# Load order and row length in a cached-attention kernel: K0 between the halves of wq, K further ahead of V, three pairs of V chunks in 32 KB rows

## The chip, the cores and the metric

One core of a Trainium2 chip. The metric is the device time of one execution in microseconds. The profile shows a span some 1.8 us shorter than that time; the stretches and moments below are in microseconds from the start of the span. The record marks each run fast or slow by its time and granted clock.

## The reference, cut to what matters

One query token per sequence, 32 sequences, 32 query heads over 8 K/V heads, a window of the last 512 cached positions, heads of 128, everything in bfloat16:

```python
q = (x @ wq).reshape(B, Sq, Hq, Dh).transpose(0, 2, 1, 3)   # x [32, 1, 512], wq [512, 4096]
k = repeat(k_cache[:, :, Sk - W:, :], 4, axis=1)            # k_cache [32, 8, 2048, 128], W = 512
v = repeat(v_cache[:, :, Sk - W:, :], 4, axis=1)
p = softmax(einsum("bhqd,bhkd->bhqk", q, k) * Dh ** -0.5)
o = einsum("bhqk,bhkd->bhqd", p, v).reshape(B, Sq, Hq * Dh) @ wo   # wo [4096, 512]
```

The used window of the two caches is 67 MB, the weights 8.4 MB. Each K and V element is used for four query rows, so there is little arithmetic per byte.

## The kernel before: the parts that matter

K and V come in 16 chunks each. A chunk is 2 MB: 128 partitions of 16 KB. Two neighbouring chunks, 2q and 2q+1, belong to the same four sequences, and in memory the two 16 KB rows of a partition touch. K has 3 buffers (`NK`), V has 4 (`NV`). wq comes in two 2 MB halves, wo at the end in 4 KB rows. All these loads go through one queue, in the order of a list, and each waits for its buffer:

```python
DMA_ORDER = (
    "K0 K1 K2 V0 K3 K4 V1 K5 K6 K7 V2 K8 K9 V3 K10 V4 K11 K12 V5 K13 K14 V6 K15 V7 V8 V9 V10 V11 V12 "
    "V13 V14 V15"
).split()
def cache_rows(cache, m):
    q, e = divmod(m, 2)
    rows = cache[4 * q:4 * q + 4, :, SK - W:, :].rearrange("b g (s r) d -> (b g) s (r d)", s=KS)
    return rows[:, :, e * CR * DH:(e + 1) * CR * DH]
...                                       # first both halves of wq, then in the order of the list:
    if name[0] == "K":
        if n >= NK:
            sp.wait_ge(dve_T, 2 * (n - NK + 1))       # both transposes of K(n-3) are done
        sp.dma_start(K_sb[:, n % NK]..., cache_rows(k_cache, n)).then_inc(sem_k[n % NK], 16)
    else:
        if n >= NV:
            sp.wait_ge(pe_PV, n - NV + 1)             # PV of V(n-4) is done
        sp.dma_start(V_sb[:, n % NV]..., cache_rows(v_cache, n)).then_inc(sem_v[n % NV], 16)
...
sp.wait_ge(pe_PV, 2 * Z_HOME.rindex("w") + 2)         # PV 11 is done: wo may overwrite w_sb
```

Every engine walks its own list. On VectorE, `Tn.b` transposes half b of chunk Kn, `Mq` and `Rq` are the row maximum and the inverse sum of a softmax, `Zq.i` is a quarter of the spread of the probabilities over a block-diagonal operand (multiplies with a mask; ScalarE does another share of it). On TensorE, `Sq` are the scores of chunks 2q and 2q+1, `Pq` turns the probabilities, `Vn` multiplies chunk Vn ("PV n"). On ScalarE, `E`, `N`, `C`, `O` are the exponential, the normalisation and two evacuations. GpSimd builds the scores' weight operand. In the profile's lines PE is TensorE (PEld its weight loads), DVE VectorE, ACT ScalarE, POOL GpSimd, and SPq the queue from which SyncE issues the loads.

Of the kernel before, what the change touches and what calls it, by code (L numbers as in the profile page):

```python
# [12 lines left out]
def bass_standalone__sliding_block_cached__sampling_kernel(  # L13
# [7 lines left out]
):  # L21
    B, Sq, D = x.shape
    _, HKV, SK, DH = k_cache.shape
    HD = wq.shape[1]
    HQ = HD // DH
# [8 lines left out]
    U32 = mybir.dt.uint32  # L34
    NK = 3
    NV = 4
# [4 lines left out]
    CR = KR // 2  # L41
# [6 lines left out]
    ZD = XD // 4  # L48
    ZA = (NBG - XD) // 4
    DMA_ORDER = (  # L50
        "K0 K1 K2 V0 K3 K4 V1 K5 K6 K7 V2 K8 K9 V3 K10 V4 K11 K12 V5 K13 K14 V6 K15 V7 V8 V9 V10 V11 V12 "
        "V13 V14 V15"
    ).split()
    PE_ORDER = (
        "S0 P0 S1 P1 V0 V1 S2 P2 V2 S3 V3 S4 P3 P4 V4 S5 V5 P5 S6 V6 P6 V7 S7 V8 V9 P7 V10 V11 V12 V13 "
        "V14 V15"
    ).split()
    DVE_ORDER = (
        "T0.0 T0.1 T1.0 T1.1 T2.0 T2.1 M0 R0 T3.0 Z0.0 T3.1 Z0.1 T4.0 M1 Z0.2 R1 T4.1 Z0.3 T5.0 T5.1 "
        "T6.0 T6.1 Z1.0 Z1.1 M2 Z1.2 R2 T7.0 Z1.3 T7.1 T8.0 T8.1 M3 T9.0 R3 T9.1 Z2.0 T10.0 M4 Z2.1 R4 "  # L60
        "T10.1 Z2.2 Z2.3 T11.0 T11.1 T12.0 T12.1 M5 R5 Z3.0 T13.0 Z3.1 T13.1 Z3.2 T14.0 M6 Z3.3 R6 T14.1 "
        "Z4.0 T15.0 Z4.1 T15.1 Z4.2 Z4.3 Z5.0 M7 Z5.1 Z5.2 R7 Z5.3 Z6.0 Z6.1 Z6.2 Z6.3 Z7.0 Z7.1 Z7.2 "
        "Z7.3"
    ).split()
    ACT_ORDER = (
        "E0 N0 C0 Z0.0 Z0.1 Z0.2 Z0.3 E1 N1 C1 O0 Z1.0 Z1.1 E2 Z1.2 N2 Z1.3 C2 E3 N3 O1 Z2.0 Z2.1 C3 E4 "
        "Z2.2 N4 Z2.3 C4 E5 N5 O2 Z3.0 C5 Z3.1 Z3.2 Z3.3 E6 N6 Z4.0 Z4.1 C6 Z4.2 Z4.3 O3 Z5.0 Z5.1 E7 "
        "Z5.2 N7 Z5.3 Z6.0 Z6.1 C7 O4 Z6.2 Z6.3 Z7.0 Z7.1 O5 Z7.2 Z7.3 O6 O7"
    ).split()
    Z_HOME = "wwwwkwtk"  # L70

    with ExitStack() as es:
        sb = lambda name, shape, dt: es.enter_context(nc.sbuf_tensor(name, shape, dt))
# [3 lines left out]
        w_sb = sb("w_sb", [P, DKT, HD], BF16)  # L77
        K_sb = sb("K_sb", [P, NK, CR, DH], BF16)
        KT_sb = sb("KT_sb", [P, NK, 2, G, CR, KS, 2], BF16)
        V_sb = sb("V_sb", [P, NV, CR, DH], BF16)  # L80
# [14 lines left out]
        Q_sb = KT_sb[:, 2].rearrange("p b i r s e -> p (b i r s e)")[:, 0:8 * DH].rearrange("p (h d) -> p h d", h=8)  # L95
# [7 lines left out]
        QW = oT_flat.bitcast(U32).rearrange("p (h k b) -> p h k b", h=8, k=2)  # L103
        QA = QA_sb[:, :, :, :, :, :].rearrange("p c h q k e -> p (c h q k e)").bitcast(U32).rearrange(
            "p (c h q k) -> p c h q k", c=4, h=8, q=NQUAD)
# [12 lines left out]
        X_ps = ps("X_ps", [P, 3, 512], F32)  # L118
# [3 lines left out]
        sem_wq = [sem(f"sem_wq{i}") for i in range(2)]  # L122
# [3 lines left out]
        sem_v = [sem(f"sem_v{i}") for i in range(NV)]  # L126
        sem_out = sem("sem_out")
        pe_xT = sem("pe_xT")
        pe_q = sem("pe_q")
        pe_S = sem("pe_S")  # L130
        pe_PT = sem("pe_PT")
        pe_PV = sem("pe_PV")
# [3 lines left out]
        dve_q = sem("dve_q")  # L136
# [6 lines left out]
        act_q = sem("act_q")  # L143
# [15 lines left out]
        wq_rows = wq.rearrange("(p t) n -> p (t n)", t=DKT)  # L159
        wq_half = DKT * HD // 2  # L160
# [9 lines left out]
        def pos_half(q, e):  # L170
            return e ^ kt_pair(q)[2]

        def z_of(q):
            return {"w": Z_w, "k": Z_k, "t": Z_t}[Z_HOME[q]]

        def z_waits(eng, q):
            if q == 0:
                eng.wait_ge(pool_mask, 3)
                eng.wait_ge(pe_q, 1)
            elif Z_HOME[q] in Z_HOME[:q]:  # L180
                eng.wait_ge(pe_PV, 2 * Z_HOME[:q].rindex(Z_HOME[q]) + 2)
            elif Z_HOME[q] == "k":
                eng.wait_ge(dve_T, 2 * NCH - 2)
            else:
                eng.wait_ge(pe_S, NQUAD)

        def cache_rows(cache, m):
            q, e = divmod(m, 2)
            rows = cache[4 * q:4 * q + 4, :, SK - W:, :].rearrange("b g (s r) d -> (b g) s (r d)", s=KS)
            return rows[:, :, e * CR * DH:(e + 1) * CR * DH]  # L190

        @block.sync
        def _(sp):
            sp.dma_start(
                w_sb[:, 2:4, :].rearrange("p k n -> p (k n)"), wq_rows[:, wq_half:]
            ).then_inc(sem_wq[1], 16)
            for name in DMA_ORDER:
                n = int(name[1:])
                if name[0] == "K":
                    if n >= NK:  # L200
                        sp.wait_ge(dve_T, 2 * (n - NK + 1))
                    sp.dma_start(  # L202
                        K_sb[:, n % NK].rearrange("p r d -> p (r d)"), cache_rows(k_cache, n)
                    ).then_inc(sem_k[n % NK], 16)
                else:
                    if n >= NV:
                        sp.wait_ge(pe_PV, n - NV + 1)
                    sp.dma_start(
                        V_sb[:, n % NV].rearrange("p r d -> p (r d)"), cache_rows(v_cache, n)
                    ).then_inc(sem_v[n % NV], 16)  # L210
            sp.wait_ge(pe_PV, 2 * Z_HOME.rindex("w") + 2)
            for hg in range(NHG):
                for i0, i1 in ((0, 4),) if hg < NHG - 1 else ((0, WO_CUT), (WO_CUT, 4)):
                    sp.dma_start(  # L214
                        wo_sb[:, hg, i0:i1].rearrange("p i n -> p (i n)"),
                        wo[hg * 512:(hg + 1) * 512, :].rearrange("(m i) n -> m (i n)", i=4)[:, i0 * 512:i1 * 512],
                    ).then_inc(sem_last if i0 else sem_wo[hg], 16)
            sp.wait_ge(dve_out, 2)
            sp.wait_ge(act_out, 2)
            sp.dma_start(  # L220
                out.rearrange("b s n -> b (s n)"), out_sb[:, :, :].rearrange("b c n -> b (c n)")
            ).then_inc(sem_out, 16)
            sp.wait_ge(sem_out, 16)
# [58 lines left out]
        def _(pe):  # L282
# [64 lines left out]
            def pv(m):  # L347
                q, e = divmod(m, 2)
                pe.wait_ge(dve_Z, q + 1)
                pe.wait_ge(act_Z, q + 1)  # L350
                if q >= 2 and e == 0:
                    pe.wait_ge(act_O, q - 1)
                pe.wait_ge(sem_v[m % NV], 16 * (m // NV + 1))
                x0 = CR * pos_half(q, e)
                for r in range(CR):
                    ins = pe.matmul(  # L356
                        O_ps[:, q % 2, 0:P],
                        lhsT=V_sb[:, m % NV, r, :],
                        rhs=z_of(q)[:, :, x0 + r, :],
                        start=(e == 0 and r == 0), stop=(e == 1 and r == CR - 1), tile_position=(0, 0),  # L360
                    )
                ins.then_inc(pe_PV, 1)
# [13 lines left out]
            for name in PE_ORDER:  # L376
                k = int(name[1:])
# [25 lines left out]
        def _(dve):  # L403
# [1 line left out]
            dve.tensor_copy(  # L405
                xT_sb[:, :, :], X_ps[:, 2, 0:DKT * 32].rearrange("p (kt b) -> p kt b", b=32)
            ).then_inc(dve_xT, 1)
            dve.wait_ge(pe_q, 1)
            dve.tensor_copy(  # L409
                Q_sb[:, 0:4, :].rearrange("p h d -> p (h d)"), X_ps[:, 0, :]  # L410
            ).then_inc(dve_q, 1)
            dve.wait_ge(dve_q, 1)
            dve.wait_ge(act_q, 1)
            dve.transpose(  # L414
                QW.rearrange("p h k b -> p (h k b)"),
                Q_sb[:, :, :].rearrange("p h d -> p (h d)").bitcast(U32),
            ).then_inc(dve_q, 1)
            dve.wait_ge(dve_q, 2)
            for a in range(4):
                for c in range(4):  # L420
                    dve.tensor_copy(  # L421
                        QA[32 * a:32 * a + 32, c],
                        QW[32 * c:32 * c + 32, :, :, a::4].rearrange("p h k q -> p h q k"),
                    ).then_inc(dve_q, 1)

            def turn(n, b):
                if b == 0:
# [32 lines left out]

            for name in DVE_ORDER:
                arg = [int(a) for a in name[1:].split(".")]
                {"T": turn, "M": top, "R": inverse, "Z": spread}[name[0]](*arg)

            def sel_evac(src, i0, ni, b0, b1):
                return (
# [111 lines left out]
```

## Time and profile before

| | before |
|---|---|
| time, median of 3 runs | 187.71 us (187.68 to 188.07) |
| span of the profile | 185.9 us |
| DMA, mean over the span | 408 GB/s |
| VectorE busy | 131.9 us (71%) |
| TensorE busy | 109.0 us (59%), granted clock 0.85 |
| packets | 6304 |

The row to read first is the busy share of the DMA engines over the 40 slices (the prediction below shows it): it stands at 9 from the second slice to the 38th. The packets of the kernel before:

```profile
DMA packets 6304, 75.80 MB, mean 408 GB/s; under 512 B 720, under 2 KB 912, under 8 KB 1936
```

34 loads of 2 MB with 128 rows each make 4352, the nine wo loads 1152, the output 32, and 44 transfers with 16 completions each 704: 6240 in the main queue, the rest is x and instructions. So a 16 KB row counts as one packet here.

### The profile page before, as it was taken

The numbers are of one execution on the slowest core, as the hardware profiler recorded it, in microseconds if no ns is written. First come the engines' busy times: TensorE is split into PE (matmuls) and PEld (weight loads), VectorE is DVE, ScalarE is ACT, GpSimd is POOL, SyncE is SP. The second block draws the span as 40 slices with busy tenths as digits, with TensorE's granted clock in tenths as the row PEclk, the third lists the DMA queues.
The fourth block names the chain that finished last, engine by engine and source line by source line (L and its number), as shares of the span: only waits on it lengthen the run. The fifth ranks groups of instructions, "written<-read, shape, count | busy, mean of one in ns | idle before, by whom it ended". The sixth has DMA issues, their size and how long they took to land.

```text
span 185.9 us, 3842 instructions
## 1 busy us (share of the span) xinstructions
PE 109.0 (59%) x1604; PEld 89.4 (48%) x1604; DVE 131.9 (71%) x239; ACT 82.3 (44%) x142; POOL 32.0 (17%) x82
## 2 busy tenths in 40 slices
PE   0232004336179906929906994159979975998752
PEld 0100001022069805819606974019949975987741
DVE  0006999689999999993699987999999995010001
ACT  3001000269320397020695018925998999910011
POOL 7100390500700080060240041000040000000000
PEclk9999999955557985885985599576999999999998
DMA  6999999999999999999999999999999999999980
GB/s 194 434 448 412 437 423 423 448 412 437 420 416 441 416 427 434 416 437 427 423 421 423 441 423 420 434 423 430 428 412 434 427 423 430 420 423 411 405 332 27
DMA packets 6304, 75.80 MB, mean 408 GB/s; under 512 B 720, under 2 KB 912, under 8 KB 1936
## 3 DMA queue, kind: packets, MB, share of 16 engines
q1 hardware_dynamic: 6240, 75.53, 96.4%
q8 instruction: 12, 0.20, 0.4%
q10 hardware_dynamic: 48, 0.03, 0.1%
q14 instruction: 4, 0.03, 0.0%
HBM read 75.53 MB, written 0.03 MB: 406 GB/s over the span
## 4 chain that ended last, share of the span: by engine, by line
DMA 64%; DVE 20%; PE 9%; issue 3%; SPq 3%; DVEq 0%
DMA V_sb<-in_v_cache_dram 31%; DMA K_sb<-in_k_cache_dram 14%; DMA w_sb<-in_wo_dram 12%; DVE KT_sb L431 12%; PE O_ps L356 8%; DMA w_sb<-in_wq_dram 6%; DVE w_sb L453 4%; DVE QA_sb L421 2%; SPq L214 2%; PE X_ps L299 1%; SPq L202 1%; DVE oT_sb L414 0%; DVE KT_sb L409 0%; PE X_ps L393 0%; DVE maxv L438 0%
## 5 line engine op out<-in xcount | busy, mean ns | idle before, releaser
L431 DVE STREAM_TRANSPOSE KT_sb<-K_sb 128x2048 uint32<-128x2048 uint32 x32 | 72.3, 2287 | 1.3 <-DMA K_sb<-in_k_cache_dram 1.1
L356 PE MATMUL O_ps<-w_sb,V_sb 128*128 128x128 bf16 x640 | 47.0, 244 | 9.6 <-DVE w_sb L453 5.0
L356 PEld LDWEIGHTS O_ps<-w_sb,V_sb 128*128 128x128 bf16 x640 | 45.6, 110 | 12.3 <-DVE w_sb L453 6.5
L268 POOL COPY QBD<-QA_sb 32x64 bf16<-32x64 bf16 x64 | 25.6, 540 | 81.2 <-PE S_ps L319 63.6
L520 ACT ACTIVATE w_sb<-PTc,mask 128x512 bf16<-128x512 bf16 x60 | 38.9, 729 | 0.0
L319 PE MATMUL S_ps<-KT_sb,QBD 128*32 128x512 bf16 x256 | 20.7, 475 | 26.6 <-DVE KT_sb L431 20.2
L453 DVE TENSOR_SCALAR w_sb<-PTc,mask 128x512 bf16<-128x512 bf16 x100 | 30.2, 370 | 6.3 <-PE O_ps L356 6.3
L319 PEld LDWEIGHTS S_ps<-KT_sb,QBD 128*32 128x32 bf16 x256 | 7.5, 110 | 36.5 <-issue 32.4
L492 ACT ACTIVATE X_ps<-S_ps,negmax 128x512 f32<-128x512 f32 x8 | 5.3, 657 | 42.8 <-DVE negmax L440 42.8
L338 PE MATMUL PT_ps<-P_bf,pick 128*128 128x128 bf16 x128 | 11.4, 260 | 17.9 <-ACT P_bf L501 14.7
L338 PEld LDWEIGHTS PT_ps<-P_bf,pick 128*128 128x128 bf16 x128 | 9.8, 119 | 20.9 <-ACT P_bf L501 16.3
L530 ACT ACTIVATE oT_sb<-O_ps 128x128 bf16<-128x128 f32 x8 | 6.0, 750 | 28.2 <-PE O_ps L356 28.2
L356 PE MATMUL O_ps<-K_sb,V_sb 128*128 128x128 bf16 x256 | 14.9, 217 | 3.5 <-DMA V_sb<-in_v_cache_dram 2.2
L356 PEld LDWEIGHTS O_ps<-K_sb,V_sb 128*128 128x128 bf16 x256 | 14.5, 96 | 4.3 <-issue 2.5
L520 ACT ACTIVATE K_sb<-PTc,mask 128x512 bf16<-128x512 bf16 x24 | 15.3, 725 | 1.6 <-DVE KT_sb L431 1.6
L453 DVE TENSOR_SCALAR K_sb<-PTc,mask 128x512 bf16<-128x512 bf16 x40 | 12.1, 377 | 0.3 <-ACT PTc L511 0.2
L474 DVE CAST K_sb<-S_ps 128x256 bf16<-128x256 f32 x1 | 0.4, 425 | 14.3 <-PE S_ps L368 14.3
L356 PE MATMUL O_ps<-KT_sb,V_sb 128*128 128x128 bf16 x128 | 7.5, 217 | 2.3 <-DMA V_sb<-in_v_cache_dram 2.3
L356 PEld LDWEIGHTS O_ps<-KT_sb,V_sb 128*128 128x128 bf16 x128 | 7.3, 96 | 2.5 <-issue 2.5
L520 ACT ACTIVATE KT_sb<-PTc,mask 128x512 bf16<-128x512 bf16 x12 | 7.7, 728 | 0.0
L501 ACT ACTIVATE P_bf<-X_ps,recip 128x512 bf16<-128x512 f32 x8 | 5.5, 684 | 4.5 <-DVE recip L446 4.4
L409 DVE CAST KT_sb<-X_ps 128x512 bf16<-128x512 f32 x1 | 0.7, 692 | 9.2 <-PE X_ps L299 9.2
(41 smaller groups left out, 49.6 us busy)
## 6 DMA issues: line engine op xcount, KB each, us to landing
K_sb<-in_k_cache_dram SPq DMA_DIRECT2D x16, 2048.0 KB, 15.1
V_sb<-in_v_cache_dram SPq DMA_DIRECT2D x16, 2048.0 KB, 16.8
w_sb<-in_wq_dram SPq DMA_DIRECT2D x2, 2048.0 KB, 9.7
w_sb<-in_wo_dram SPq DMA_DIRECT2D x7, 512.0 KB, 19.8
w_sb<-in_wo_dram SPq DMA_DIRECT2D x1, 384.0 KB, 22.6
w_sb<-in_wo_dram SPq DMA_DIRECT2D x1, 128.0 KB, 14.4
oT_sb<-in_x_dram ACTq DMA_DIRECT2D x1, 32.0 KB, 4.4
out_dram<-oT_sb SPq DMA_DIRECT2D x1, 32.0 KB, 1.5
```

Source lines behind the costliest of these rows:

```text
L214: sp.dma_start(wo_sb[:, hg, i0:i1].rearrange("p i n -> p (i n)"), wo[hg * 512:(hg + 1) * 512, :].rearrange("(m i) n -> m (i n)", i=4)[:, i ...
L268: pool.tensor_copy(dst[:, i, :, x0:x0 + 4], src).then_inc(pool_qbd, 1)
L319: ins = pe.matmul(S_ps[32 * c:32 * c + 32, q % 2, :], lhsT=QBD[:, q % 2, g, b, e, :], rhs=bass.AP(tensor=KT_sb, offset=s0 * slot + (b * G ...
L338: ins = pe.matmul(PT_ps[:, r, :], lhsT=pick[:, r, KS - s:KS - s + P], rhs=P_bf[:, s, :], start=(s == 0), stop=(s == KS - 1), tile_position ...
L356: ins = pe.matmul(O_ps[:, q % 2, 0:P], lhsT=V_sb[:, m % NV, r, :], rhs=z_of(q)[:, :, x0 + r, :], start=(e == 0 and r == 0), stop=(e == 1 a ...
L421: dve.tensor_copy(QA[32 * a:32 * a + 32, c], QW[32 * c:32 * c + 32, :, :, a::4].rearrange("p h k q -> p h q k"),).then_inc(dve_q, 1)
L431: dve.transpose(KT_w[:, n % NK, b].rearrange("p i r s -> p r i s"), K_w[:, n % NK, :, 32 * b:32 * b + 32],).then_inc(dve_T, 1)
L453: ins = dve.tensor_scalar(z_of(q)[:, k].rearrange("p x r -> p (x r)"), PTc[:, q % RING].rearrange("p x r -> p (x r)"), mask[:, k:k + 1], N ...
L492: act.activation(P_f32, S_ps[:, q % 2, :], ACTF.Exp, bias=negmax[:, q:q + 1], scale=SCALE, accum_out=sums[:, q:q + 1],).then_inc(act_exp, 1)
L501: act.activation(P_bf[:, :, :], P_f32.rearrange("p (x s) -> p s x", s=KS), ACTF.Copy, scale=recip[:, q:q + 1],).then_inc(act_P, 1)
L520: ins = act.activation(z_of(q)[:, k].rearrange("p x r -> p (x r)"), PTc[:, q % RING].rearrange("p x r -> p (x r)"), ACTF.Copy, scale=mask[ ...
L530: act.activation(oT_sb[:, :, 4 * q:4 * q + 4].rearrange("p h a -> p a h"), O_ps[:, q % 2, 0:P].rearrange("p (a h) -> p a h", a=4), ACTF.Co ...
```

## The change

Its intent: let VectorE transpose K0 while the second half of wq is still on its way; run K further ahead so that VectorE waits for it less; and load V2/3, V4/5, V6/7 as pairs, in rows of 32 KB. The lists of all engines are arranged anew to fit. The core of the diff (the lists of TensorE and ScalarE are cut; theirs are reorderings alone):

```diff
     DMA_ORDER = (
-        "K0 K1 K2 V0 K3 K4 V1 K5 K6 K7 V2 K8 K9 V3 K10 V4 K11 K12 V5 K13 K14 V6 K15 V7 V8 V9 V10 V11 V12 "
-        "V13 V14 V15"
+        "K0 B0 K1 V0 K2 K3 K4 K5 V1 K6 K7 K8 V2 K9 K10 K11 V4 K12 K13 K14 V6 K15 V8 V9 V10 V11 V12 V13 V14 "
+        "V15"
     DVE_ORDER = (
-        "T0.0 T0.1 T1.0 T1.1 T2.0 T2.1 M0 R0 T3.0 Z0.0 T3.1 Z0.1 T4.0 M1 Z0.2 R1 T4.1 Z0.3 T5.0 T5.1 "
+        "T0.0 T0.1 Q0 T1.0 T1.1 T2.0 M0 T2.1 R0 T3.0 T3.1 Z0.0 T4.0 M1 Z0.1 T4.1 R1 Z0.2 T5.0 Z0.3 T5.1 T6.0 "
 [cut: the rest of this list, those of TensorE and ScalarE]
+    V_PAIRED = (2, 4, 6)
-        def cache_rows(cache, m):
+        def cache_rows(cache, m, k=1):
-            return rows[:, :, e * CR * DH:(e + 1) * CR * DH]
+            return rows[:, :, e * CR * DH:(e + k) * CR * DH]
-            sp.dma_start(w_sb[:, 2:4, :]..., wq_rows[:, wq_half:]).then_inc(sem_wq[1], 16)
             for name in DMA_ORDER:
+                if name[0] == "B":
+                    sp.dma_start(w_sb[:, 2:4, :]..., wq_rows[:, wq_half:]).then_inc(sem_wq[1], 16)
-                    if n >= NV:
-                        sp.wait_ge(pe_PV, n - NV + 1)
+                    k = 2 if n in V_PAIRED else 1
+                    if n + k > NV:
+                        sp.wait_ge(pe_PV, n - NV + k)
-                        V_sb[:, n % NV]..., cache_rows(v_cache, n)
+                        V_sb[:, n % NV:n % NV + k]..., cache_rows(v_cache, n, k)
```

The query work on VectorE became an entry of the list, `Q0`, after T0.1. TensorE waits for a pair once, at its first chunk.

## The prediction

> **What bounds the kernel now.** I read the page's slices first, then stretches of time, then the chain of waits, then the times to landing, and last the timeline of VectorE.
>
> ```profile
> DVE  0006999689999999993699987999999995010001
> DMA  6999999999999999999999999999999999999980
> GB/s 194 434 448 412 437 423 423 448 412 437 420 416 441 416 427 434 416 437 427 423 421 423 441 423 420 434 423 430 428 412 434 427 423 430 420 423 411 405 332 27
> HBM read 75.53 MB, written 0.03 MB: 406 GB/s over the span
> ```
>
> From the second slice to the 38th all 16 DMA engines are full. VectorE is nearly full too, but only in the middle. The same in long stretches (the columns after the five engines are granted clock, DMA share, GB/s):
>
> ```profile
> 20.00:70.00 50.00, 21.79 (x256) 15.18 (x256) 46.97 (x64) 17.99 (x32) 16.50 (x40) 0.78 1.00 425
> 70.00:120.00 50.00, 32.52 (x416) 27.83 (x416) 42.95 (x59) 23.72 (x43) 9.12 (x24) 0.74 1.01 427
> 120.00:160.00 40.00, 32.75 (x511) 28.79 (x512) 35.72 (x101) 33.40 (x57) 1.97 (x2) 0.92 1.01 425
> 172.00:179.00 7.00, 4.68 (x100) 4.42 (x104) 0.42 (x1) 0.72 (x1) 0.00 (x0) 1.00 1.01 404
> ```
>
> There is no hole in 20 to 160 us: the share is 1.00 or more and the rate 425 to 427 GB/s. The last line is the stretch that loads wo, in 4 KB rows instead of 16 KB rows: the engines are as full and move less. Pieces of the chain, in order of time (start, length):
>
> ```profile
> 1.26 11.95 DMA w_sb<-in_wq_dram
> ...
> 26.04 11.64 DMA K_sb<-in_k_cache_dram
> ...
> 136.08 15.97 DMA V_sb<-in_v_cache_dram
> ...
> 160.04 22.62 DMA w_sb<-in_wo_dram
> 182.67 0.04 issue
> ```
>
> It goes from transfer to transfer; the wo load ends at 182.67 and 3.2 us of fixed tail follow (last matmuls, copies, the output). The chain also names VectorE, for it follows the issue of a load back to the wait that held it. That does not make VectorE the bound, since the issued load still has a queue in front of it. Time from issue to landing (K first, then V):
>
> ```profile
> DMA to landing us min/median/max: 10.7/15.1/24.8
> DMA to landing us min/median/max: 15.0/16.8/29.4
> ```
>
> One 2 MB chunk takes about 4.95 us: the first half of wq is used at 8.4 us, V11, the 30th of the 2 MB loads, at 152.05, and (152.05 - 8.4) / 29 = 4.95. So even the most urgent K load (10.7) found 5.7 us of other loads, latency included, ahead of it. Bound: the transfer of 75.53 MB, with spare time at every issue.
>
> [...] five mask multiplies take 1.36 us, but beside GpSimd's copies (47.34 to 51.02 us) they took
>
> ```profile
> 48.11 2.59 DVE L453 TENSOR_SCALAR w_sb<-PTc,mask 128x512 bf16<-128x512 bf16 x5
> ```
>
> **The change part by part.** Bytes, matmuls, transposes and spreads are all kept; only transfers and orders change.
>
> Rows of 32 KB. Per engine and GB/s: a 16 KB row costs 16384 B / (425/16 GB/s) = 617 ns, a 4 KB row 4096 / (404/16) = 162 ns, the share of a completion packet included (both kinds have 8 rows per engine and load). The difference, 455 ns for 12288 B, is 0.0370 ns per byte; 162 - 152 leaves about 10.5 ns fixed per row. Three pairs each save 8 rows per engine and one completion packet (within that 10.5): 3 x 8 x 10.5 ns = 0.25 us. [...] This lies on the bound[...].
>
> K0 between the halves of wq. A straight swap: K0 lands at about 13.3 instead of 18.3, the second half at 18.3 instead of 13.2. VectorE does two transposes (2 x 2.26 = 4.5 us) in a time in which it was idle, and the query work (0.69 + 0.71 + 4.80 = 6.2 us) starts at 18.3 + 1.9 = 20.2 instead of 15.2, ending at 26.4 rather than 21.5. After it two transposes are left before scores 0 instead of four: start at 26.4 + 4.5 = 30.9 against 30.55 before. Worth nothing at the end.
>
> K further ahead of V. With 3 K buffers, load Kn waits for the transposes of K(n-3). I replayed the new lists by hand with the durations of the trace (transpose half 2.26, scores 3.6 at half clock and 2.0 at full, PV 4.6 and 3.8, spread quarter 1.36 or 2.6 beside GpSimd), and set each issue against the moment at which the queue would run dry (load j lands at 8.4 + 4.95(j - 1)):
> - K4 is released after T1.1 at 30.9; the queue lasts until K3 lands at 38.1: 7 us spare.
> - K5 after T2.1: K2 lands at 33.2, T2.0 35.4, top of scores 36.2, T2.1 38.5; until 43.1: 4.6 spare.
> - K7 after T4.1 at about 52.4; until 57.9: 5.5 spare.
> - K8 after T5.1: 52.4 + 0.1 + 1.4 + 2.3 + 1.3 + 2.3 = 59.8; until K7 lands at 62.9: 3.1 spare. The tightest.
> - K9 after T6.1 at about 64; the first V pair lasts until 77.7: 13 spare.
> - K10 to K15 have 9 to 16 spare, as each has a V or V pair ahead.
> - Pair V4/V5 needs PV 1 (about 68), pair V6/V7 needs PV 3 (about 91); their turns to be issued are at about 79 and 103, after the K loads before them. The double wait costs nothing.
> - V10, behind pair V6/V7, needs PV 6: the pair lands at about 127.3, PV 6 ends at 131.5; the queue lasts until 142: 10 spare.
>
> No issue is late, so the gain or loss here is 0. From V11 on the order is the old one: PV 11 follows its landing at 152, then V15 and wo are issued behind 15 us of queue, as before.
>
> Sum: 187.71 - 0.3 = 187.4 us.
>
> **The rivals.** (a) The DMA queue runs dry early. Loads K2 to K5 are now in one run on three buffers, and issue takes 0.53 us plus some latency. For it: K8's 3.1 us and K5's 4.6 us are thinner than the 5.7 us of the kernel before, and TensorE ran at half clock at 39 to 57 us. Against: the durations are measured, and half-clock times are already in the replay. A miss of 1 to 2 us there would never be regained: 188.5 to 189.5 us. (b) VectorE becomes the bound. It is busy for 46.97 of 50 us at 20 to 70. But its total is 131.9 us, spread over some 140, and the change adds nothing and uses 4.5 us of early idle time; after about 80 my replay has it wait for K9. If it held the last spreads back beyond the landing of V15 at about 172, 189 or more; there are some 15 us between. (c) Larger rows help more than extrapolated, or the earlier K removes a hidden starvation. For it: the author paired just these loads. Against: the share is already 1.00[...].
>
> **Range and chances.** Centre 187.4. Below it, (c) and run-to-run spread (187.68 to 188.07 for one kernel) reach 186.8; above, a short starvation or a slower sample reaches 188.4. Faster by over 2% needs under 183.96, which the bytes forbid at the measured rate: 1%. Slower by over 2% needs 3.8 us of empty queue, more than any miss of the replay I can name: 2%. Within 2%: 97%.
>
> **What would show it.** Right: the DMA row stays 9 throughout; the rate in 20 to 160 us stays 425 to 428, highest where pairs move; packets fall by 3 x (128 + 16) = 432 from 6304 to 5872, if a 32 KB row is one packet; the shortest K landing drops to about 8 us (K8 or K5) without a dip of the share; VectorE transposes at about 13 us, and scores 0 start near 31; the wo load still ends the chain, 3.2 us before the end. Wrong: a slice below 9 between 20 and 170 us, a K landing under 6 us, or a packet count still near 6304. More than 1 us gained would mean that I mis-sized the fixed cost per row; more than 1 us lost, a dry queue that the replay missed.

Passages that rested on figures or rules which no trace or run shows are cut out, as marked. Two of them bear on the forecast. One was an upper case for the gain of the rows, above the 0.25 us worked out from 10.5 ns per row; the sum takes 0.3 us, between the two, and comes to 187.4 us. Without the cut term it would be 187.71 - 0.25 = 187.46 us. The other was a ceiling on what any change of loads could gain, so against rival (c) only the DMA share of 1.00 is left.

## The result, and the profile after

| | before | after |
|---|---|---|
| time, median of 6 runs each | 187.70 us (187.51 to 188.07) | 187.46 us (187.26 to 187.63) |
| ratio after / before, 95% interval | | 0.9983 (0.997 to 0.9996) |
| span of the profile | 185.9 us | 185.7 us |
| packets | 6304 | 5872 |

A ratio here is the mean time of one kernel's fast runs over that of the other's of the same rounds, so it is not quite the ratio of the medians. 0.9983 of 187.7 us is 0.3 us less. The page of the changed kernel (VectorE, DMA share, rate, packets):

```profile
DVE  0018696999999999939999489999999946510001
...
DMA  6999999999999999999999999999999999999980
...
DMA packets 5872, 75.80 MB, mean 408 GB/s; under 512 B 672, under 2 KB 864, under 8 KB 1888
```

The DMA row is the same, digit for digit. 432 packets are gone, which is 3 x (128 rows + 16 completions), so a row of 32 KB is one packet too. The three stretches of the prediction, changed kernel (start and end, length, busy us and instructions of PE, PEld, DVE, ACT and POOL, granted clock, DMA share, GB/s):

```profile
20.00:70.00 50.00, 23.39 (x292) 16.44 (x292) 46.90 (x66) 16.00 (x29) 15.46 (x40) 0.90 1.01 429
70.00:120.00 50.00, 29.57 (x404) 23.73 (x400) 42.77 (x69) 25.13 (x44) 9.34 (x24) 0.77 1.00 428
120.00:160.00 40.00, 32.52 (x488) 28.81 (x481) 35.16 (x100) 34.65 (x60) 1.98 (x2) 0.84 1.00 423
```

425 became 429, 427 became 428 and 425 became 423 GB/s (over the whole of 20 to 160 us: 426 before, 427 after). This is not a gain in one stretch and a loss in another: a row counts each packet whole where it starts, so the 32 KB packets in flight at 70 and 120 us shift bytes over the border. With each packet of the packed traces spread over its own duration, the three are 426.8, 427.0 and 425.7 before, and 427.0, 428.4 and 426.2 after: little more, and most in the stretch where most of the pairs move. The end of its chain of waits:

```profile
161.09 21.45 DMA w_sb<-in_wo_dram
182.53 0.04 issue
```

The wo load ends at 182.53 instead of 182.67, with the same tail behind it. What did change inside is the work of VectorE and TensorE. Timeline of VectorE, then the first scores on TensorE (columns: start, length, operation, and in brackets the idle time before it and what ended it):

```profile
13.20 4.50 DVE L436 STREAM_TRANSPOSE KT_sb<-K_sb 128x2048 uint32<-128x2048 uint32 x2 [7.22 <-DMA K_sb<-in_k_cache_dram]
...
21.54 4.78 DVE L426 COPY QA_sb<-oT_sb 32x128 uint32<-32x128 uint32 x16
...
83.20 4.50 DVE L436 STREAM_TRANSPOSE KT_sb<-K_sb 128x2048 uint32<-128x2048 uint32 x2 [3.12 <-DMA K_sb<-in_k_cache_dram]
```

```profile
31.01 3.61 PE L321 MATMUL S_ps<-KT_sb,QBD 128*32 128x512 bf16 x32 [10.99 <-POOL QBD L270]
```

K0 is transposed at 13.2 in time that was idle, and VectorE is so far ahead by 80 us that it waits 3.1 us for K9. None of it moves the end. A warning lies in the chain of waits by engine, before and then after:

```profile
DMA 64%; DVE 20%; PE 9%; issue 3%; SPq 3%; DVEq 0%
```

```profile
DMA 45%; PE 22%; DVE 20%; issue 6%; SPq 4%; ACT 0%; DVEq 0%
```

The DMA's share fell by 19 points and TensorE's rose by 13, with the same bound and nearly the same time. The chain goes from a load back to whatever released its issue, even where that issue came early; its shares say nothing of the spare time in between.

### The profile page after: what moved, and what is told of

It reads as the page before. It is cut to its first block, busy times and chain, and to the rows that moved or that the text cites. A ratio compares the mean times of both kernels' runs of the same rounds, so it can differ in the third digit from the quotient of the medians.

```text
span 185.7 us, 3839 instructions
## 1 busy us (share of the span) xinstructions
PE 108.6 (58%) x1604; PEld 88.0 (47%) x1604; DVE 131.4 (71%) x239; ACT 82.6 (44%) x142; POOL 31.2 (17%) x82
## 2 busy tenths in 40 slices
DMA packets 5872, 75.80 MB, mean 408 GB/s; under 512 B 672, under 2 KB 864, under 8 KB 1888
## 4 chain that ended last, share of the span: by engine, by line
DMA 45%; PE 22%; DVE 20%; issue 6%; SPq 4%; ACT 0%; DVEq 0%
DMA K_sb<-in_k_cache_dram 26%; PE O_ps L360 14%; DVE KT_sb L436 12%; DMA w_sb<-in_wo_dram 12%; DMA V_sb<-in_v_cache_dram 8%; PE S_ps L321 7%; DVE w_sb L458 6%; SPq L216 2%; DVE maxv L443 2%; PE PT_ps L340 1%; SPq L210 1%; SPq L203 1%; SPq L197 0%; ACT P_bf L506 0%; PE X_ps L397 0%
## 5 line engine op out<-in xcount | busy, mean ns | idle before, releaser
L360 PE MATMUL O_ps<-w_sb,V_sb 128*128 128x128 bf16 x640 | 42.1, 230 | 3.7 <-DVE w_sb L458 3.1
L360 PEld LDWEIGHTS O_ps<-w_sb,V_sb 128*128 128x128 bf16 x640 | 40.8, 103 | 6.1 <-DVE w_sb L458 3.9
L321 PE MATMUL S_ps<-KT_sb,QBD 128*32 128x512 bf16 x256 | 22.3, 504 | 18.1 <-POOL QBD L270 11.0
L340 PE MATMUL PT_ps<-P_bf,pick 128*128 128x128 bf16 x128 | 12.6, 277 | 29.8 <-ACT P_bf L506 25.5
L340 PEld LDWEIGHTS PT_ps<-P_bf,pick 128*128 128x128 bf16 x128 | 10.9, 128 | 33.5 <-ACT P_bf L506 28.3
L458 DVE TENSOR_SCALAR K_sb<-PTc,mask 128x512 bf16<-128x512 bf16 x40 | 10.7, 347 | 4.4 <-ACT PTc L516 4.4
L360 PE MATMUL O_ps<-KT_sb,V_sb 128*128 128x128 bf16 x128 | 9.1, 240 | 2.5 <-DMA V_sb<-in_v_cache_dram 2.5
L360 PEld LDWEIGHTS O_ps<-KT_sb,V_sb 128*128 128x128 bf16 x128 | 8.9, 108 | 2.6 <-issue 2.6
L301 PE MATMUL X_ps<-w_sb,oT_sb 128*32 128x512 bf16 x32 | 3.8, 626 | 10.6 <-DMA w_sb<-in_wq_dram 10.6
L516 ACT ACTIVATE PTc<-PT_ps 128x512 bf16<-128x512 f32 x8 | 4.8, 594 | 10.5 <-PE PT_ps L340 10.5
```

What stands on the lines that cost most here:

```text
L301: ins = pe.matmul(X_ps[32 * c:32 * c + 32, k, :], lhsT=xT_sb[:, kt, :], rhs=w_sb[:, kt, c * 1024 + k * 512:c * 1024 + (k + 1) * 512], star ...
L321: ins = pe.matmul(S_ps[32 * c:32 * c + 32, q % 2, :], lhsT=QBD[:, q % 2, g, b, e, :], rhs=bass.AP(tensor=KT_sb, offset=s0 * slot + (b * G ...
L340: ins = pe.matmul(PT_ps[:, r, :], lhsT=pick[:, r, KS - s:KS - s + P], rhs=P_bf[:, s, :], start=(s == 0), stop=(s == KS - 1), tile_position ...
L360: ins = pe.matmul(O_ps[:, q % 2, 0:P], lhsT=V_sb[:, m % NV, r, :], rhs=z_of(q)[:, :, x0 + r, :], start=(e == 0 and r == 0), stop=(e == 1 a ...
L458: ins = dve.tensor_scalar(z_of(q)[:, k].rearrange("p x r -> p (x r)"), PTc[:, q % RING].rearrange("p x r -> p (x r)"), mask[:, k:k + 1], N ...
L516: act.activation(PTc[:, q % RING], PT_ps[:, :, :].rearrange("p r x -> p x r"), ACTF.Copy).then_inc(act_PT, 1)
```

## The experiments

Theories. Mine: the bytes and the fixed cost per row set the end; orders are worth nothing as long as each load is issued in time. Rival A: the new orders removed a hidden starvation, and the rows are worth nothing. Rival B: VectorE is the bound. Each run was timed in five rounds beside the kernel before on the same chip.

**e1_order_only** and **e2_pairs_only**: one part of the change each.

```diff
# e1, on the changed kernel
-    V_PAIRED = (2, 4, 6)                   + "V2 V3", "V4 V5", "V6 V7" in DMA_ORDER
+    V_PAIRED = ()
# e2, on the changed kernel: the lists of the kernel before (Q0 first), and
+    DMA_ORDER = "B0 K0 K1 K2 V0 K3 K4 V1 K5 K6 K7 V2 K8 K9 K10 V4 K11 K12 K13 K14 V6 K15 V8 V9 ... V15"
```

> The changed kernel with all its orders, but V in single 16 KB rows (V2 V3, V4 V5, V6 V7 one after the other). My theory (DMA transfer is the bound, the gain is fixed cost per row): the gain of the change is gone, ratio to the kernel before 0.9995 to 1.0005, DMA packets 6304 as before. Rival A (the orders removed a hidden starvation, rows are worth nothing): ratio 0.998 to 0.9985, as the whole change. Rival B (VectorE is the bound): gain kept as in A.

> The operation lists and the wq order of the kernel before, with only V2/3, V4/5, V6/7 loaded as pairs in place of the first of each. My theory: the whole gain, [...] ratio 0.998 to 0.9987, packets 5872, no dip of the DMA share (K8 and K9 land 5 us later than before, which I expect no wait of the DMA queue from). Rival A (orders made the gain): ratio 1.000, or above if the old order starves with pairs.

Measured: e1 187.58 us, ratio 0.9998 (0.9987 to 1.001), 6304 packets; e2 187.43 us, ratio 0.9992 (0.998 to 1.0005), 5872 packets, no dip of the DMA share in either. Both point the way of my theory, the orders doing nothing and the pairs a little, but e2's mean lies outside the range that I expected, and the intervals overlap each other and that of the change. A difference of 0.3 us is too small for the times. The rates of the traces separate better: over 20 to 160 us, with packets spread over their durations, 426.5 GB/s before, 426.6 in e1, 427.4 in e2 and 427.3 in the changed kernel. 0.8 of 426.5 over 140 us is 0.26 us, with the pairs and not with the orders; but these are single traces. So I also took a larger dose.

**e3_v_8kb_rows** and **e12_v_4kb_rows**: the dose the other way. Each V chunk of the kernel before comes as two transfers of 8 KB rows, or four of 4 KB rows.

```diff
-sp.dma_start(V_sb[:, n % NV]..., cache_rows(v_cache, n))
+for h in range(2):                                             # e12: 4
+    sp.dma_start(V_sb[:, n % NV, h * CR // 2:(h + 1) * CR // 2]...,
+                 cache_rows(v_cache, n)[:, :, h * CR * DH // 2:(h + 1) * CR * DH // 2])
```

> The kernel before with each V chunk loaded as two transfers of 8 KB rows: 16 x (8 rows + 1 completion) more packets per engine. My theory: 16 x 8 x 10.5 ns = 1.34 us longer[...], ratio 1.005 to 1.010, packets 6304 + 16 x 144 = 8608. Rival (rows of 8 KB and more cost the same per byte, the gain of the change is not from rows): ratio 1.000, within 0.3 us.

> The dose of e3_v_8kb_rows tripled: each V chunk of the kernel before as four transfers of 4 KB rows, 16 x 24 = 384 more rows per engine instead of 128. If the cost is a constant per row (8.6 ns by e3_v_8kb_rows), 3.3 us more (2.6 to 4.0 by that run's interval), ratio 1.014 to 1.021. If rows of 8 KB lost for another reason than their count (the halves of a row interleaved across transfers, say), no such line: clearly more than 5 us or no more than about 1.5 us.

Measured: e3 188.80 us, ratio 1.0059 (1.0047 to 1.0071), 1.1 us for 128 more rows per engine; e12 191.07 us, ratio 1.0175 (1.016 to 1.0189), 3.3 us for 384. Both give 8.6 ns per row (187.6 x 0.0059 / 128 and 187.86 x 0.0175 / 384): a straight line. The packets of the traces, read one by one, carry it on to 32 KB: the median one took 160 ns with 4 KB (e12), 312 with 8 KB (e3), and 613 with 16 KB and 1216 with 32 KB (changed kernel). Two of 16 KB less one of 32 KB is 10 ns, the row that a pair saves. The stretches of e12:

```profile
20.00:70.00 50.00, 21.25 (x256) 15.04 (x256) 46.97 (x64) 17.98 (x32) 15.85 (x40) 0.80 1.01 422
70.00:120.00 50.00, 30.62 (x416) 25.88 (x416) 42.90 (x59) 23.92 (x43) 9.10 (x24) 0.81 1.01 417
120.00:160.00 40.00, 32.49 (x480) 28.42 (x480) 35.85 (x100) 30.94 (x53) 1.98 (x2) 0.85 1.02 410
```

The share stays at 1.01 to 1.02, and the rate falls from 425, 427 and 425 GB/s in the kernel before to 422, 417 and 410, most in 120 to 160 us, where nearly all that comes is V: here the busy share of the DMA engines did not tell rows that carry from fixed cost.

**e9_v_in_two** and **e10_v_odd_even**: e3 and e12 added completions as well as rows. These two add completions alone, with two transfers of 64 partitions per chunk and 16 KB rows.

```diff
+for h in range(2):
+    e9:  sp.dma_start(V_sb[64 * h:64 * h + 64, n % NV]..., cache_rows(v_cache, n)[16 * h:16 * h + 16])
+    e10: sp.dma_start(V_sb[h::2, n % NV]..., cache_rows(v_cache, n)[:, h::2])
```

> The kernel before with each V chunk loaded as two transfers of 64 partitions, rows of 16 KB kept: only 16 x 16 more completion packets and 16 more issues, against e3_v_8kb_rows, which had these and 16 x 128 more rows for +1.1 us. If the fixed cost sits in the rows: within 0.3 us of the kernel before. If it sits in the completion of a transfer: about +1.1 us, ratio 1.006. I lean to rows, at two to one.

> The kernel before with each V chunk as two transfers, one of the even, one of the odd partitions, so that (unlike in e9_v_in_two, where 64 neighbouring partitions halved the rate to some 225 GB/s) all of the buffer is reached by each. Rows of 16 KB kept, 16 x 16 more completion packets. If the 1.15 us of e3_v_8kb_rows sits in the rows: within 0.3 us of the kernel before; if in the completions: about +1.1 us, ratio 1.006. If the odd and even split halves the rate too: tens of us more, and nothing is learned of the completions.

Measured: e9 271.35 to 275.17 us in its three fast runs (276.49 is the median of all six, three of them slow), ratio 1.4579, a miss by some 86 us that had nothing to do with completions. While it loads only V:

```profile
170.00:210.00 40.00, 20.26 (x264) 18.51 (x261) 21.81 (x62) 18.27 (x32) 1.97 (x2) 0.79 1.01 224
```

A share of 1.01 at 224 GB/s: transfers into 64 neighbouring partitions moved about half of the 425 to 427 GB/s of the kernel before, whose transfers go into 128. Why, no run shows. e10, with the same number of partitions spread over the whole buffer, ran at the rate of the kernel before, 425 to 427 GB/s in the three stretches: 187.46 us, ratio 0.9991 (0.9978 to 1.0004). By the upper end of that interval, 256 more completion packets cost at most 0.08 us. So the 1.1 us of e3 lies in the rows, not in the completions or in the number of transfers.

**e4_half_v8**: fewer bytes. Half of each row of V8 is not loaded (a wrong result).

```diff
+if n == 8:
+    sp.dma_start(V_sb[:, n % NV, 0:CR // 2]..., cache_rows(v_cache, n)[:, :, 0:CR * DH // 2])
```

> The changed kernel with only the first half of each row of V8 loaded (1 MB less; wrong result on purpose, the other half of the buffer keeps older data). No engine has less work. My theory (bytes set the end): half a chunk less, 4.95 / 2 = 2.5 us shorter than the changed kernel, so 2.8 us or 1.5% under the kernel before. Rival B (VectorE or another engine sets the end): no change against the changed kernel, ratio 0.998.

Measured: 185.09 us, ratio 0.9862 (0.9849 to 0.9875). 0.9983 - 0.9862 = 0.0121, or 2.3 us less than the changed kernel for 1 MB. At that place in the list, the bytes set the end.

**d1_delay1, d4_delay4, d2_late**: what a late issue costs, and whether VectorE's time does. One, four or two repeated transposes are put into VectorE's list, each with its own wait.

```diff
 def turn(n, b):
+    for i in range(1 if (n, b) == (5, 1) else 0):     # d4: 4; d2_late: 2 at (8, 1)
+        [wait for the transpose before, repeat transpose (n, 0) with the same result, wait for it]
```

> The changed kernel with one more transpose of K5 (2.26 us, a repeat of the same result) ahead of the second half of its transpose, so the issue of K8, the tightest of my replay (3.1 us spare; the trace of the changed kernel has it at 58.8, its predecessor K7 landing near 63.5), comes 2.3 us later. My theory: still in time, no change, ratio to the kernel before 0.997 to 0.9995, shortest K landing about 9.7 - 2.3 = 7.4 us. Rival B (VectorE is the bound): 2.3 us more than the changed kernel, ratio 1.0105.

> The same with four more transposes, 9.0 us. My theory: K8 is issued at about 67.8, after the queue ran dry at about 63.5; the loss is 4.3 us plus the latency from issue to first bytes[...], 5.8 to 6.8 us over the changed kernel, ratio 1.029 to 1.035, a hole in the DMA share at 63 to 71 us, none later as all later issues had 9 us and more to spare. Rival B: 9.0 us more, ratio 1.046. If issues never mattered: ratio 0.998.

> The changed kernel with two more transposes (a repeat of K8's first half, 4.5 us) on VectorE, now ahead of the second half of K8's transpose, which releases K11. There the queue is long: K11 is issued at 77.4 in the trace of the changed kernel, K10 ahead of it has its last bytes at about 86. d1_delay1 and d4_delay4 cost nearly what rival B (VectorE is the bound) foresaw, so this tells the two apart. My theory (a late issue of one load costs, not VectorE's time): no change, ratio to the kernel before 0.997 to 0.9995, no hole in the DMA share. Rival B: 4.5 us more than the changed kernel, ratio 1.022.

Measured: d1 189.23 us, ratio 1.0079 (1.0062 to 1.0096); d4 196.35 us, ratio 1.0453 (1.0434 to 1.0471); d2_late 187.67 us, ratio 1.0024 (0.9994 to 1.0055). I had expected no loss from d1 and 5.8 to 6.8 us from d4 (4.3 us and a time from issue to first bytes whose figure, not shown by any run, is cut; the trace of d4 has 1.3 us below); both missed. Taken alone, d1 and d4 look like rival B: 1.0079 - 0.9983 is 1.8 us for a transpose of 2.3 us, and 1.0453 - 0.9983 is 8.8 us for four. d2_late speaks against that, as e4 does: 4.6 us more work on VectorE, 20 us later in its list, cost 0.8 us at the mean, mostly from two of its six runs (188.90 and 189.35; the other four lie at 187.37 to 187.95), not 4.5 us. I had expected at most 0.9995; its interval reaches above that, and what slowed the two runs is open. The time around K9 in d2_late and, for comparison, above in the changed kernel:

```profile
76.33 4.64 DVE L439 STREAM_TRANSPOSE KT_sb<-K_sb 128x2048 uint32<-128x2048 uint32 x2
...
85.90 4.50 DVE L444 STREAM_TRANSPOSE KT_sb<-K_sb 128x2048 uint32<-128x2048 uint32 x2
```

VectorE takes K9 2.7 us later and without the 3.1 us of waiting: part of the padding went into time that had been idle. In this trace (of the run with 187.95) no load behind it left the DMA engines idle, but two came near it: K11 was issued at 83.4 instead of 77.4 and V10 at 138.3 instead of 133.2, and around 86 and 140 us some packets took up to 1.8 and 1.4 us instead of 0.61. So what d2_late did cost may again be late issues; that is not shown. In d4, on the contrary, the queue ran dry. The queue's own timeline in the changed kernel, d1 and d4 (three K issues, the last of which, K8, takes the final 0.53 us), then the DMA of d4 by the microsecond:

```profile
42.56 16.80 SPq L203 DMA_DIRECT2D K_sb<-in_k_cache_dram  x3
...
42.60 19.33 SPq L204 DMA_DIRECT2D K_sb<-in_k_cache_dram  x3
...
43.02 26.35 SPq L204 DMA_DIRECT2D K_sb<-in_k_cache_dram  x3
```

```profile
61.00:62.00 1.00, 1.00 (x21) 1.00 (x19) 0.96 (x2) 0.00 (x0) 0.00 (x0) 1.00 0.39 164
62.00:63.00 1.00, 0.39 (x7) 0.22 (x4) 1.00 (x1) 0.00 (x0) 0.00 (x0) 1.00 0.04 16
...
69.00:70.00 1.00, 1.00 (x12) 0.40 (x15) 1.00 (x1) 0.00 (x0) 0.00 (x0) 0.50 0.00 0
70.00:71.00 1.00, 1.00 (x13) 0.35 (x8) 1.00 (x2) 0.00 (x0) 0.00 (x0) 0.50 1.19 279
71.00:72.00 1.00, 1.00 (x16) 0.35 (x8) 1.00 (x2) 0.00 (x0) 0.00 (x0) 0.50 0.69 295
72.00:73.00 1.00, 1.00 (x14) 0.56 (x7) 1.00 (x1) 0.00 (x0) 0.41 (x2) 0.50 1.09 459
```

The 16 engines did not run out together: by the packets of d4 they finished K7, the load ahead of K8, between 61.2 and 62.8, at 61.8 in the mean. K8's issue began at 43.02 + 26.35 - 0.53 = 68.8, its first packet started at 70.16, 1.3 us later, and the first 16 packets at 70.4 in the mean; these took 1.13 us instead of 0.61 (279 and 295 GB/s in the rows). So an engine lost some 70.4 - 61.8 + 0.5 = 9.1 us, and the span grew by 195.0 - 185.7 = 9.3: nothing was made up.

**e7_seven_pairs** and **e8_more_pairs**: more of what gained. e7 also pairs V8/9 to V14/15; e8 pairs V8/9, V10/11 and, of K, K10/11 and K12/13.

```diff
-    V_PAIRED = (2, 4, 6)
+    V_PAIRED = (2, 4, 6, 8, 10, 12, 14)                     # e7
+    V_PAIRED = (2, 4, 6, 8, 10); K_PAIRED = (10, 12)        # e8; a K pair waits for both of its buffers
-    "... V6 V7 V8 S7 V9 ..."                                 # TensorE
+    "... V6 V7 S7 V8 V9 ..."
```

> The changed kernel with V8/9, V10/11, V12/13 and V14/15 as pairs too (and scores 7 ahead of PV 8 on TensorE). By the 9 ns per row that e3_v_8kb_rows showed, four more pairs save 4 x 8 x 9 ns = 0.29 us: 187.15, ratio 0.9965 to 0.9975, if the queue holds. But V12/13 can be issued only when PV 9 is done (about 149.8) and the queue runs dry at 152; V14/15 at 160 against 162: up to 0.5 us can be lost at each, then ratio 0.998 to 1.002 and dips of the DMA share there.

> The changed kernel with V8/9 and V10/11 and, of K, K10/11 and K12/13 as pairs too (seven in all, none among the last four V loads; scores 7 ahead of PV 8 on TensorE). Four more pairs at 9 ns per row: 4 x 8 x 9 ns = 0.29 us less than the changed kernel, about 187.2, ratio 0.996 to 0.9975, packets 5296. In e7_seven_pairs the pair V14/15 at the very end and the late issue of V12/13 cost 4 to 5 us; here V12 to V15 come singly. If a pair's double wait costs by itself, as against its place: 1 us or more lost, ratio above 1.003.

Measured: e7 192.37 us (median of six, one of them slow), ratio 1.0213 (1.0187 to 1.0239); e8 191.16 us, ratio 1.0192 (1.0174 to 1.021). Both of my expectations missed by 4 to 5 us. In e7, the last chunks on TensorE:

```profile
175.42 8.98 PE L359 MATMUL O_ps<-K_sb,V_sb 128*128 128x128 bf16 x128 [2.36 <-DMA V_sb<-in_v_cache_dram]
```

V14 and V15 land as one, so the two multiplications run from 175.4 to 184.4, in part at a granted clock of 0.57; in the changed kernel the last one ended at 172.82 + 3.77 = 176.6. The queue also ran low before it (336 and 262 GB/s in 148 to 152 us, while V12/13 waited for PV 9; it was empty for moments near 140 and 163 us too). In e8 the trace shows a K pair and a V pair doing harm together:

```profile
93.20 2.31 DVE L440 STREAM_TRANSPOSE KT_sb<-K_sb 128x2048 uint32<-128x2048 uint32 x1 [5.52 <-DMA K_sb<-in_k_cache_dram]
```

```profile
140.00:142.00 2.00, 2.00 (x40) 2.00 (x38) 2.00 (x7) 0.64 (x2) 0.00 (x0) 1.00 0.30 123
142.00:144.00 2.00, 0.96 (x19) 0.71 (x20) 2.00 (x3) 1.35 (x3) 0.33 (x1) 1.00 0.24 66
```

K10, in a pair, lands a whole chunk later: its transpose starts at 93.2 instead of 88.1. Everything after it slid; PV 7 ended at 142.6 instead of 136.8, and V10/11, which had to wait for it, left the queue dry at 140 to 144. A single V10 would have waited only for PV 6, which ended at 139.0, 3.6 us sooner. How much of the loss the K pairs make by themselves no run shows. No run here beats the changed kernel beyond its interval.

## Why the prediction was right

- **The bound** held: the DMA row stayed at 9 from the second slice to the 38th, the wo load still ends the chain, half a chunk of bytes less took 2.3 us off (e4), and 4.6 us more work on VectorE cost 0.8 us at the mean where the queue was long (d2_late).
- **The fixed cost per row** was put at 10.5 ns. e3 and e12 measured 8.6 ns. By that, 24 rows per engine are worth 24 x 8.6 = 0.21 us, or 0.24 by the 10 ns of the packets, against 0.25 by 10.5 ns, 0.3 in the prediction's sum, and 0.3 (0.08 to 0.56) measured for the whole change. That 187.4 was so near to 187.46 is partly luck: the measurement does not resolve the gain so well. The prediction counted a completion packet within its figure; by e10 that part is near nothing (at most 0.08 us for 256 of them).
- **The swap of K0** went as worked out: transposes at 13.2 (13.3 predicted), query done at 26.3 (26.4), scores 0 at 31.0 (30.9), nothing at the end. The wait before scores 0 was ended by GpSimd's weight operand, though, 0.1 us after the transposes (26.36 + 4.50 = 30.86) that the prediction names; it does not mention GpSimd there.
- **No issue too late** was right, but its margin was mis-sized, and that is the one step that failed. For K8 the prediction says 3.1 us spare. d1 and d4 show about 1: K8's issue, by the rows of the queue's timeline above, moved from 42.56 + 16.80 - 0.53 = 58.8 in the changed kernel to 42.60 + 19.33 - 0.53 = 61.4 in d1 and to 68.8 in d4, 2.6 and 10.0 us, and the loss was 1.8 and 8.8. The term that was wrong is the moment at which the queue runs dry. I took it from the landing of K7, which comes only when the last of the 16 engines is done: 62.9 by the clock of the prediction, 63.7 in the changed kernel (up to that, K8 would have had 4.8 us). By the packets of the changed kernel the engines finish K7 between 61.26 and 63.21, at 61.7 in the mean. And I left out the 1.33 us from the start of the issue to the first packet (d4; the same in d1); my issue time was 1.0 us too late, which hid some of it. 61.26 - 58.82 - 1.33 = 1.1 us until the first engine would stand idle. That the change lost nothing here was partly luck. Rival (a) of the prediction was much nearer than it looked: the new order has this one load within about a microsecond of a loss, and being 2.6 us late cost six times what the pairs gain.
- **Smaller misses:** the shortest K landing was 9.7 us, not about 8, and two stretches left the range of 425 to 428 GB/s, 20 to 70 us with 429 and 120 to 160 us with 423; counted by the packets' durations, both are inside it.

What stays open: the division of the 0.3 us between orders and pairs was not resolved by the times of e1 and e2; it rests on the row cost from e3, e10 and e12, on the packets' durations and on one trace each of e1 and e2.

## What to carry to other kernels

With the DMA row at 9 from the second slice to the 38th, reordering bought nothing that could be measured here (e1, ratio 0.9998); 1 MB less took 2.3 us off (e4), and a row cost 8.6 ns per engine (e3, e12; about 10 by the packets of 16 and 32 KB), so count bytes and rows before going to work. Longer rows by pairing had a price: in e8 the first half landed one chunk later (K10's transpose at 93.2 instead of 88.1), and V10/11, which needs two free buffers, waited for PV 7, done 3.6 us after PV 6; so pair only where nobody waits for the first half. Reckon the spare time of an issue up to the moment when the first DMA engine runs out (61.26 for K7 here), not up to the landing of the load ahead (63.7), and take off the time from issue to first bytes (1.33 us in d4); the surest test is to delay that one issue on purpose, and the same delay elsewhere.
